# The V side of two more head pairs loaded row by row, in a fused attention and two-MLP kernel, with the attention list written anew

## The chip, the cores and the metric

The kernel runs on one core of a Trainium2 chip. The metric is the device time of one execution in microseconds, the median of several runs. One execution was also recorded by the hardware profiler, and every row shown below is from that one.

## The reference

Three stages follow one another; the change lies in the first. q, k and v have 2 batches, 8 heads, 768 positions and a head size of 64.

```python
k_sum = k.reshape(B, H, nb, 32, D).max(axis=3)       # 24 block summaries of the keys
v_sum = v.reshape(B, H, nb, 32, D).mean(axis=3)      # 24 block means of the values
scores_l = scale * q @ k^T                           # kept where |i - j| < 16
scores_s = scale * q @ k_sum^T + log(32)
a = softmax(concat([scores_l masked, scores_s]))
out = a @ concat([v, v_sum])
```

The result, as x of shape (2, 768, 512), goes through a token MLP over the 768 positions (`w_tok1`, 256 wide, and `w_tok2`), a channel MLP (512 to 1536 to 512), and then a layer norm with another channel MLP (512 to 2048 to 512), each with its residual.

## The kernel before, in words

**Pairs, windows and groups.** Two heads that follow one another make a pair; there are 8 pairs (i = 0 to 7; 0 to 3 are batch 0). A pair has 12 windows of 64 queries. A window sees 96 keys and 24 block summaries, 120 columns in all (`NK`). Four windows make a group; group n belongs to pair n // 3, so there are 24 groups.

**One group.** `q` (`att_qk`, L459) makes the scores on TensorE, 16 small matmuls; `m` (`att_min`, L479) adds the mask and takes the row minimum on VectorE, four instructions; `e` (`att_exp`, L500) is the exponential on ScalarE, four instructions; `t` (`att_tr`, L508) transposes the four probability blocks on TensorE; `c` (`att_evac`, L516) copies them out of PSUM on ScalarE; `a` (`att_av`, L522) multiplies them with V, 16 small matmuls; `n` (`att_norm`, L540) divides, on VectorE. All the scores live in one PSUM tile, of which groups of even and odd n use alternate strips.

**K.** `l` (`load_pair`, L322) loads K and Q of a pair. `k` (`prep_k`) takes the block maxima on VectorE; `K` copies them beside the keys with ScalarE, `J` does the same with GpSimd.

**V, first way, pairs below `NT`.** `v` (`load_vt`, L346) loads V with the head sizes on the partitions, 128 x 6 x 160, into a tile of `wide` (named VW). The block means are summed either by VectorE (`s`, L393 to L399) and written by ScalarE (`S`, L420 to L428), or summed by GpSimd (`p`, `sum_v`, L379) and written by GpSimd (`T`, `mean_v`, L409) or by ScalarE (`S`). Then TensorE turns the pair round in three groups `w` (`att_vtr`, L444) of four transposes each, and each group is copied out of PSUM into the tile V by ScalarE (`x`) or VectorE (`X`) (`att_vev`, L453).

**V, second way, the other pairs.** `r` (`load_v`, L352) loads V twice over with positions on the partitions, already cut into windows: two DMAs of 96 partitions x 6 x 136 numbers, with ones beside the values. `v` (L350) also loads the plain turned V, 128 x 768, into the tile VT. `s` (`prep_v1`, L400 to L407) sums the blocks there with GpSimd: four additions that halve the width, and two that write the sums into Z. `S` (L429, L430) is one transpose of Z on TensorE; `z` (`prep_v3`, L432) scales and copies it out with ScalarE into the single tile zs; `u` (`prep_v4`, L436) writes the means into the 12 windows of V with two GpSimd copies.

**Buffers.** V has three tiles (i % 3), K and Q three (i % 3), VT two (i % 2), zs one, and `stage`, into which `h` (`load_half`, L207) loads a weight block of 512 KB, three. `W` and `D` decode such a block (ScalarE, then VectorE), `C` and `O` split it into two halves. `g`, `G` and `H` are steps of the token MLP and of the transposes after it, which TensorE does between the groups; an entry `g` with a number below 4 or of 10, 11, 20 or 21 is 12 matmuls of 256 columns (`g1`, L556), and `g4` to `g9` are 12 matmuls of 512 columns each (`g2`, L575). `f` is a matmul on zeros, put in where nothing else can be done.

**The order.** `FRONT` (L49 to L63) is a list of such letters with their numbers. `attention` (L1119) walks it once, and each engine's instructions, the DMA queue of SyncE among them, keep the order of the list. So an entry that waits holds up all the later ones of its engine, and no engine's work moves past another entry of its own. When the list is through, the channel MLPs follow (`run`, from L1251).

Of the kernel before, what the change touches and what calls it, by code (L numbers as in the profile page):

```python
# [44 lines left out]
EARLY = 16  # L45
NEG = -8e9
EPS = 1e-9
NT = 4
FRONT = """  # L49
d0 f d1 f j0 f y0 f j1 f y1 f i0 v0 f i1 f l1 f K0 f v1 q0 l2 f f m0 f f e0 f h1 q1 t0 m1 f c0 f q2  # L50
e1 f m2 f l3 e2 t1 s0 f f f v2 t2 k1 S0 h2 w1 v3 w0 K1 x1 h0 q3 X0 c1 w2 m3 p1 a0 e3 q4 n0 c2 t3 m4
x2 a1 e4 k2 q5 T1 a2 n1 K2 c3 w3 m5 W1 t4 x3 D1 q6 c4 a3 e5 n2 w5 m6 w4 x5 t5 x4 n3 q7 p2 c5 k3 a4
e6 m7 a5 e7 t6 n4 r4 q8 n5 J3 S2 p3 t7 c6 m8 h4 w7 W2 y2 w6 X7 c7 q9 l4 e8 X6 a7 D2 v4 a6 S3 W0 v5
n7 w11 l5 w9 m9 x11 t8 x9 w8 D0 c8 q10 x8 w10 n6 e9 g1 X10 W4 k4 D4 K4 s4 t9 m10 C4 g0 c9 O4 G1 e10
H1 s5 q11 G0 H0 t10 l6 m11 S4 a8 e11 k5 q12 h3 z4 t11 c10 h7 n8 u4 a9 h5 m12 v7 e12 a10 n9 r5 J5 q13
n10 c11 t12 m13 a11 c12 k6 e13 q14 S5 a12 J6 m14 z5 e14 u5 t13 n12 q15 n11 c13 t14 W3 m15 a13 W7 D3
q16 e15 g2 m16 e16 s7 n13 D7 C3 c14 t15 O3 C7 q17 c15 t16 m17 G2 a14 e17 H2 q18 n14 r7 c16 a15 m18
e18 a16 l7 n15 q19 n16 W5 g3 h6 D5 v6 h8 m19 C5 h9 e19 r6 O5 t17 t18 G3 c17 q20 H3 k7 c18 g7 m20 K7
e20 g5 H7 W6 q21 H5 s6 g8 m21 e21 D6 S7 g6 W8 H8 h10 C6 D8 z7 t19 W9 u7 S6 g4 z6 O6 h11 H6 u6 q22 H4
g9 m22 e22 q23 H9 a18 m23 b g19 n18 g12 G19 a17 G12 H19 t20 H12 c19 g13 n17 c20 g16 t21 G16 a19 G13  # L60
H16 e23 a20 H13 n19 g11 c21 n20 t23 G11 g15 H11 t22 G15 g14 c22 H15 a21 G14 g18 c23 n21 a22 G18 H14
a23 n22 g10 n23 H18 g20 G10 H10 g21 G20 H20 P17 G21 G17 H21 H17
"""  # L63
SCALE = 1.0 / math.sqrt(D)

# [5 lines left out]
class Kern:  # L71
# [274 lines left out]
    def load_vt(self, i):  # L346
        if i < NT:
            self.nc.sync.dma_start(self.wide[i][:, 0:6, NB : NB + 160], self.vk[i])
        else:
            self.nc.sync.dma_start(self.VT[i % 2], self.vt[i - NT])  # L350

    def load_v(self, i):  # L352
        nc = self.nc
        if i < NT:
            return
        V = self.V[i % 3].rearrange("p (j w) c -> p j w c", j=2)
        nc.sync.dma_start(V[NB:NK, 0], self.v[i - NT, 0])
        nc.sync.dma_start(V[0:96, 1], self.v[i - NT, 1])

    def value(self, i, w):  # L360
        return self.V[i % 3][:, w if i < NT else 6 * (w % 2) + w // 2]

# [1090 lines left out]
```

## Time and profile before

| | |
|---|---|
| median of 3 runs | 559.36 us (558.47 to 559.53) |
| profiled execution | 558.98 us, its span 557.2 us |
| TensorE busy | 549.6 us (99%) |
| VectorE busy | 403.1 us (72%) |
| ScalarE busy | 272.3 us (49%) |
| GpSimd busy | 35.3 us (6%), all of it in the first 74 us |
| moved by DMA | 135.74 MB, mean 244 GB/s |
| granted TensorE clock | 1.00 of full speed |

Busy time of TensorE counts the pipelined length of each matmul, so two matmuls that overlap are busy once, and what one adds to the time is read from the start of one group to the start of the next.

### The profile page before, as it was taken

Reading aid. Unit: us, or ns where it says so; the run is one execution under the profiler, and the core shown is the slowest. Engines: PE = TensorE matmul, PEld = TensorE weight load, DVE = VectorE, ACT = ScalarE, POOL = GpSimd, SP = SyncE. Lnnn points to the kernel's source line nnn. Section 1 sums busy time; section 2 is a strip of 40 time slices with the busy share of each in tenths; the row PEclk is TensorE's granted clock in tenths of the full one; section 3 lists DMA queues with packets and bytes.
Section 4 is the critical chain, followed back from the end, with each engine's and each line's share of the span. In section 5 each row is a group of like instructions: output and inputs, shape, how many; then the busy total and the mean of one; then the engine's idle time right before and its main releaser. Section 6 shows DMA issues by size and latency. Waiting matters only on the chain.

```text
span 557.2 us, 10264 instructions
## 1 busy us (share of the span) xinstructions
PE 549.6 (99%) x3673; PEld 495.4 (89%) x3674; DVE 403.1 (72%) x977; ACT 272.3 (49%) x602; POOL 35.3 (6%) x66
## 2 busy tenths in 40 slices
PE   8999999999999999999999999999999999999997
PEld 4877779899899898999999998888998999999997
DVE  5989864657776887655669957888866776677781
ACT  5979653237754645454787325463422223334320
POOL 3554320000000000000000000000000000000000
PEclk9999999999999999999999999999999999999999
DMA  8977920425888879898656995897787898777555
GB/s 257 336 245 240 309 79 2 151 78 193 256 283 296 291 270 311 287 308 304 241 204 231 303 329 179 288 331 261 251 310 229 282 322 257 236 240 241 176 156 184
DMA packets 63810, 135.74 MB, mean 244 GB/s; under 512 B 5776, under 2 KB 23056, under 8 KB 63760
## 3 DMA queue, kind: packets, MB, share of 16 engines
q1 hardware_dynamic: 63760, 135.09, 72.8%
q8 instruction: 29, 0.48, 0.4%
q14 instruction: 21, 0.17, 0.1%
HBM read 100.47 MB, written 34.60 MB: 242 GB/s over the span
## 4 chain that ended last, share of the span: by engine, by line
PE 88%; DMA 4%; ACT 3%; POOL 2%; DVE 1%; issue 1%; SPq 0%; POOLq 0%; DVEq 0%; ACTq 0%
PE m L319 8%; PE m L318 8%; PE m L317 8%; PE acc_x L318 4%; PE acc_x L319 4%; PE acc_x L317 4%; PE g L560 3%; PE acc_y L319 2%; PE acc_y L318 2%; PE acc_y L317 2%; ACT pr L504 2%; DMA VT<-in_vt_dram 1%; DMA stage<-in_wts_dram 1%; PE acc_m L319 1%; PE acc_m L318 1%; PE acc_m L317 1%
## 5 line engine op out<-in xcount | busy, mean ns | idle before, releaser
L317 PE MATMUL m<-slot,slot 128*128 128x384 f32 (+1 forms) x136 | 45.8, 337 | 0.0
L319 PE MATMUL m<-slot,slot 128*128 128x384 f32 (+1 forms) x136 | 45.4, 334 | 0.0
L318 PE MATMUL m<-slot,slot 128*128 128x384 f32 (+1 forms) x136 | 45.4, 334 | 0.0
L319 PE MATMUL acc_x<-slot,al 128*128 128x512 f32 x96 | 37.8, 394 | 0.0
L318 PE MATMUL acc_x<-slot,ah 128*128 128x512 f32 x96 | 37.8, 394 | 0.0
L317 PE MATMUL acc_x<-slot,ah 128*128 128x512 f32 x96 | 37.5, 391 | 0.0
L504 ACT ACTIVATE pr<-sn,mn 128x120 f32<-128x120 f32 x96 | 29.8, 389 | 5.3 <-DVE mn L489 5.3
L317 PEld LDWEIGHTS m<-slot,slot 128*128 128x128 f32 x136 | 25.6, 188 | 1.8
L318 PEld LDWEIGHTS m<-slot,slot 128*128 128x128 f32 x136 | 25.6, 188 | 1.6
L165 DVE SCALAR_TENSOR_TENSOR dec<-stage,dec 128x512 uint32<-128x512 uint32 x36 | 25.1, 696 | 0.7
L319 PEld LDWEIGHTS m<-slot,slot 128*128 128x128 f32 x136 | 25.5, 188 | 0.0
L142 ACT ACTIVATE dec<-stage 128x512 f32<-128x512 f32 x36 | 24.3, 675 | 1.0 <-DMA stage<-in_wts_dram 1.0
L489 DVE CUSTOM_DVE_ANT_0 sn<-scores,mask 128x120 f32<-128x120 f32 x96 | 21.3, 277 | 3.7 <-DMA mask<-in_mask_dram 2.0
L560 PE MATMUL g<-u,tok 128*128 128x256 f32 x96 | 22.1, 383 | 0.0
L856 ACT ACTIVATE ah<-sm 128x384 fp32r<-128x384 f32 x16 | 8.4, 523 | 28.1 <-DVE sm L866 28.1
L688 ACT ACTIVATE f_B<-tx,gt 128x384 f32<-128x384 f32 x16 | 9.3, 582 | 25.4 <-PE tx L684 25.4
L319 PEld LDWEIGHTS acc_x<-slot,al 128*128 128x128 f32 x96 | 18.0, 188 | 4.0
L319 PE MATMUL acc_y<-slot,al_s 128*128 128x256 f32 x72 | 20.1, 280 | 0.0
L318 PE MATMUL acc_y<-slot,ah_s 128*128 128x256 f32 x72 | 20.1, 279 | 0.0
L560 PEld LDWEIGHTS g<-u,tok 128*128 128x128 f32 x96 | 17.8, 190 | 2.6 <-issue 0.3
L651 ACT ACTIVATE xn<-u,nb,rs 128x128 f32<-128x128 f32 x48 | 20.1, 482 | 0.0
L317 PE MATMUL acc_y<-slot,ah_s 128*128 128x256 f32 x72 | 20.0, 278 | 0.0
(1506 smaller groups left out, 1729.2 us busy)
## 6 DMA issues: line engine op xcount, KB each, us to landing
stage<-in_wts_dram SPq DMA_DIRECT2D x62, 512.0 KB, 4.4
slot<-w1s SPq DMA_DIRECT2D x94, 256.0 KB, 3.7
w1s<-sps SPq DMA_DIRECT2D x16, 512.0 KB, 4.6
w2s<-sp SPq DMA_DIRECT2D x16, 512.0 KB, 3.3
slot<-w2s SPq DMA_DIRECT2D x16, 512.0 KB, 4.7
w2t<-wk SPq DMA_DIRECT2D x16, 512.0 KB, 4.9
slot<-w2t SPq DMA_DIRECT2D x8, 768.0 KB, 5.2
slot<-w2s SPq DMA_DIRECT2D x22, 256.0 KB, 4.6
```

The lines of the kernel that those rows point to most:

```text
L142: fold = lambda out: nc.scalar.activation(out, high, AF.Prelu, scale=2.0**-112, alpha=-(2.0**32))
L165: put(m, t[:, :, 0], 29, m, op0=ALU.logical_shift_right, op1=ALU.bitwise_or)
L317: nc.tensor.matmul(out, lhs[0], rhs[0], start=first, stop=False)
L318: nc.tensor.matmul(out, lhs[0], rhs[1], start=False, stop=False)
L319: nc.tensor.matmul(out, lhs[1], rhs[0], start=False, stop=last)
L489: nc.vector.tensor_tensor_reduce(sn[:, u], ps[:, u % 2, u // 2, :NK], self.mask[:, mv], scale=-SCALE, scalar=3e38, op0=ALU.add, op1=ALU.mi ...
L504: self.nc.scalar.activation(self.pr[n][:, u], sn[:, u], AF.Exp, bias=mn[:, u : u + 1], scale=-1.0)
L560: nc.tensor.matmul(ps[:, :256], self.tok1(st, t), self.u[:, b * ST + st, 256 * hf : 256 * hf + 256], start=st == 0, stop=st == ST - 1,)
L651: nc.scalar.activation(xn[:, j], self.u[:, g * GT + j, cc * P : cc * P + P], AF.Identity, bias=nb[:, j : j + 1], scale=rs[:, j : j + 1],)
L688: nc.scalar.activation(x, ps[:, :GN], AF.Copy, scale=self.gt[:, cc : cc + 1])
L856: nc.scalar.activation(ah, x, AF.Relu)
```

## The change

`NT` goes from 4 to 2, so pairs 2 and 3 take the second way for V, and `FRONT` is another list. Gone from the list are `w6` to `w11` and their copies, `p2`, `p3` and the entries that served them; new are `r2`, `r3`, `s2`, `s3`, `z2`, `z3`, `u2`, `u3`; `S2` and `S3` stand for another thing, the transpose. `K1` and `K4` become `J1` and `J4`. The host's layout follows `NT`.

```diff
-NT = 4
+NT = 2
 FRONT = """
-d0 f d1 f j0 f y0 f j1 f y1 f i0 v0 f i1 f l1 f K0 f v1 q0 l2 f f m0 f f e0 f h1 q1 t0 m1 f c0 f q2
-e1 f m2 f l3 e2 t1 s0 f f f v2 t2 k1 S0 h2 w1 v3 w0 K1 x1 h0 q3 X0 c1 w2 m3 p1 a0 e3 q4 n0 c2 t3 m4
-x2 a1 e4 k2 q5 T1 a2 n1 K2 c3 w3 m5 W1 t4 x3 D1 q6 c4 a3 e5 n2 w5 m6 w4 x5 t5 x4 n3 q7 p2 c5 k3 a4
-e6 m7 a5 e7 t6 n4 r4 q8 n5 J3 S2 p3 t7 c6 m8 h4 w7 W2 y2 w6 X7 c7 q9 l4 e8 X6 a7 D2 v4 a6 S3 W0 v5
-n7 w11 l5 w9 m9 x11 t8 x9 w8 D0 c8 q10 x8 w10 n6 e9 g1 X10 W4 k4 D4 K4 s4 t9 m10 C4 g0 c9 O4 G1 e10
-H1 s5 q11 G0 H0 t10 l6 m11 S4 a8 e11 k5 q12 h3 z4 t11 c10 h7 n8 u4 a9 h5 m12 v7 e12 a10 n9 r5 J5 q13
-n10 c11 t12 m13 a11 c12 k6 e13 q14 S5 a12 J6 m14 z5 e14 u5 t13 n12 q15 n11 c13 t14 W3 m15 a13 W7 D3
-q16 e15 g2 m16 e16 s7 n13 D7 C3 c14 t15 O3 C7 q17 c15 t16 m17 G2 a14 e17 H2 q18 n14 r7 c16 a15 m18
-e18 a16 l7 n15 q19 n16 W5 g3 h6 D5 v6 h8 m19 C5 h9 e19 r6 O5 t17 t18 G3 c17 q20 H3 k7 c18 g7 m20 K7
-e20 g5 H7 W6 q21 H5 s6 g8 m21 e21 D6 S7 g6 W8 H8 h10 C6 D8 z7 t19 W9 u7 S6 g4 z6 O6 h11 H6 u6 q22 H4
-g9 m22 e22 q23 H9 a18 m23 b g19 n18 g12 G19 a17 G12 H19 t20 H12 c19 g13 n17 c20 g16 t21 G16 a19 G13
-H16 e23 a20 H13 n19 g11 c21 n20 t23 G11 g15 H11 t22 G15 g14 c22 H15 a21 G14 g18 c23 n21 a22 G18 H14
-a23 n22 g10 n23 H18 g20 G10 H10 g21 G20 H20 P17 G21 G17 H21 H17
+d0 f d1 f j0 f y0 f j1 f y1 f i0 v0 f i1 f l1 f K0 f v1 q0 f v2 f m0 f l2 f e0 f f q1 h1 t0 m1 f c0
+f f e1 q2 f m2 f l3 e2 t1 f s0 r2 c1 t2 k1 S0 w1 v3 J1 w0 x1 h2 q3 X0 a1 p1 m3 a0 e3 n1 q4 n0 c2 t3
+w2 m4 c3 s2 x2 k2 q5 e4 a2 m5 K2 t4 r3 n2 W1 q6 T1 e5 D1 S2 h0 w3 w5 z2 m6 h4 x3 u2 t5 c4 X5 a3 e6
+k3 q7 w4 c5 n3 J3 t6 x4 m7 a5 e7 a4 n5 s3 q8 c6 n4 t7 m8 a6 W2 q9 e8 D2 S3 v5 z3 m9 t8 c7 u3 l4 c8
+a7 n6 e9 q10 l5 n7 a8 m10 W0 t9 v4 e10 D0 q11 r5 c9 m11 t10 s5 e11 g0 h3 n8 r4 W4 k4 c10 h7 D4 l6 J4
+t11 G0 q12 C4 H0 v7 g1 O4 h5 m12 y2 e12 k5 s4 q13 G1 H1 a9 m13 a10 e13 n9 q14 J5 n10 c11 S4 t12 z4
+m14 t13 u4 c12 a11 e14 q15 n11 S5 c13 t14 m15 z5 g2 W3 u5 e15 D3 W7 C3 D7 t15 G2 q16 H2 C7 a13 O3
+a12 c15 m16 g3 s7 e16 n13 n12 c14 k6 W5 D5 q17 J6 G3 t16 H3 C5 a14 m17 a15 e17 r7 n14 q18 n15 c16
+t17 h8 m18 a16 c17 l7 e18 a17 n16 q19 v6 n17 t18 r6 m19 g11 e19 O5 h6 c18 h11 W8 g7 G11 D8 S7 t19 H7
+h10 z7 u7 q20 c19 H11 k7 g8 m20 K7 s6 e20 g5 H8 q21 H5 g6 m21 e21 S6 g4 H6 W6 z6 D6 u6 q22 H4 C6 h9
+g9 m22 e22 a19 H9 a18 n19 q23 n18 b g12 O6 g19 G12 t20 G19 H12 t21 c20 H19 g13 c21 m23 a20 G13 a21
+e23 H13 g16 n20 g18 G16 n21 t23 G18 t22 H16 c23 H18 g15 c22 a23 G15 W9 a22 H15 n23 g14 g10 n22 G14
+H14 g20 G10 H10 g21 G20 H20 P17 G21 G17 H21 H17
 """
```

## Rows read from the trace of the kernel before

**Rows 1.** Windows by stage: length, then busy time of each engine with its instructions.
```profile
core 0: us, PE busy (x) PEld busy (x) DVE busy (x) ACT busy (x) POOL busy (x), PEclk, DMA share, GB/s
...
40.00:54.00 14.00, 13.30 (x225) 10.25 (x217) 13.10 (x67) 12.48 (x36) 6.93 (x13) 1.00 0.77 251
54.00:74.00 20.00, 18.93 (x206) 14.50 (x206) 17.59 (x74) 12.98 (x36) 9.18 (x14) 1.00 0.82 262
...
93.10:557.20 464.10, 460.91 (x2580) 426.88 (x2579) 333.62 (x674) 208.58 (x431) 0.00 (x0) 1.00 0.74 248
```
**Rows 2.** Waits of TensorE to 93 us: total us, times, longest.
```profile
PE vtr L450 <- ACT VW L422: 0.9, 2, 0.8
PE scores L470 <- POOL VT L404: 0.7, 1, 0.7
PE psv L430 <- POOL Z L407: 0.6, 1, 0.6
```
**Rows 3.** Timeline of TensorE: start us, length, instruction, operands, count.
```profile
19.44 0.64 PE L470 MATMUL scores<-K,Q 64*64 64x120 f32 x16
...
25.45 1.09 PE L450 MATMUL vtr<-ident,VW 128*120 128x128 f32 x8
26.47 0.64 PE L470 MATMUL scores<-K,Q 64*64 64x120 f32 x16
...
29.07 1.09 PE L450 MATMUL vtr<-ident,VW 128*120 128x128 f32 x8 [0.75 <-ACT VW L422]
30.00 0.60 PE L513 MATMUL pt<-ident,pr 128*120 128x128 f32 x4
30.44 0.63 PE L450 MATMUL vtr<-ident,VW 128*120 128x128 f32 x4
30.99 0.64 PE L470 MATMUL scores<-K,Q 64*64 64x120 f32 x16
...
44.49 0.32 PE L430 MATMUL psv<-ident,Z 128*120 128x128 f32 x1
44.75 0.69 PE L532 MATMUL av<-V,PT 121*64 121x65 f32 x16
```
**Rows 4.** Timeline of GpSimd, 16 to 71 us.
```profile
16.81 0.63 POOL L410 TENSOR_SCALAR VW<-vs 128x168 f32<-128x168 f32 x1
...
34.53 3.03 POOL L404 TENSOR_TENSOR VT<-VT 128x384 f32<-128x384 f32 x4 [5.88 <-DMA VT<-in_vt_dram]
37.64 0.41 POOL L407 TENSOR_TENSOR Z<-VT 128x24 f32<-128x24 f32 x2
...
67.37 1.06 POOL L407 TENSOR_TENSOR Z<-VT 128x24 f32<-128x24 f32 x2
68.38 2.18 POOL L442 COPY V<-zs 24x768 f32<-24x768 f32 x2
```
**Rows 5.** Chain that ended last, 53 to 75 us: start, length, link.
```profile
56.12 8.14 DMA VT<-in_vt_dram
...
72.02 1.37 POOL V L442
...
73.43 0.68 PE av L532 x14
```
**Rows 6.** Timeline of SyncE's DMA queue.
```profile
53.54 0.31 SPq L357 DMA_DIRECT2D V<-in_v_dram  x1
```
**Rows 7.** Windows of 5 us, columns as in the first group.
```profile
30.00:35.00 5.00, 5.00 (x46) 4.26 (x45) 4.17 (x11) 3.94 (x11) 0.47 (x1) 1.00 1.06 379
35.00:40.00 5.00, 5.00 (x64) 4.01 (x66) 3.42 (x20) 3.80 (x12) 4.53 (x9) 1.00 0.19 68
```
**Rows 8.** Timeline of VectorE around 52 us.
```profile
51.23 0.69 DVE L243 TENSOR_TENSOR slot<-dec,slot 128x512 fp32r<-128x512 f32 x1
52.19 1.15 DVE L243 TENSOR_TENSOR slot<-dec,slot 128x512 fp32r<-128x512 f32 x1 [0.27 <-ACT slot L222]
53.26 0.27 DVE L489 CUSTOM_DVE_ANT_0 sn<-scores,mask 128x120 f32<-128x120 f32 x1
```

## Prediction

> **What bounds the kernel now.** I read the windows by stage first, since one share over the whole span would mix the attention with the MLPs [rows 1]. From 93 us to the end TensorE is busy 460.9 of 464.1 us, and the view of waits has no entry of TensorE for that stretch. So the MLPs run at TensorE's pace, and whatever the attention's end gains or loses comes out at the end of the kernel, one for one. Only the first 93 us need an argument. There TensorE is nearly full too: 13.3 of 14 us between 40 and 54, 18.9 of 20 between 54 and 74. VectorE stands beside it with 13.1 of 14 us in the first of these, so two engines are near their limit at once. The waits of TensorE came next [rows 2]: 0.9 us for the mean of a V tile, 0.7 for scores, 0.6 for the sums Z. Then its timeline, for what a step costs from start to start [rows 3]; then GpSimd's and the queue's, because the change moves work there [rows 4 to 7].
>
> The front is thus a sum: TensorE's work plus its waits. Work that leaves TensorE shortens it fully, if no new wait takes its place.
>
> **What is removed.** Six groups of four transposes go, w6 to w11. From start to start, w7 and w6 took 26.47 - 25.45 = 1.02 us, w11 and w9 30.00 - 29.07 = 0.93, w8 30.99 - 30.44 = 0.55 [rows 3]: 2.50 us for five, 0.5 each, so **-3.0 us** for six. Their copies out of PSUM (four on ScalarE, two on VectorE net) go too; what these free is counted below with the order. The wait of w11 for the mean of pair 3 has no successor of its kind, as there is no such mean to wait for: **-0.8** (the longer of the two waits of 0.9 in sum [rows 2]; the rest, before w1, stays).
>
> **What is added on TensorE.** Two transposes of Z, S2 and S3. One took 44.75 - 44.49 = 0.26 us [rows 3]: **+0.5**.
>
> **The last V of the chain.** The end of the front hangs on pair 6 before the change: its VT is issued at 56.12, takes 8.14 us to land, is summed, and its means reach V at 73.4, when a18 starts [rows 5]. The queue could not issue it sooner, because r7 ahead of it waited until 53.54 for a14 to free pair 4's V [rows 6]. In this chain u7 stands between the sums s6 and u6, and holds GpSimd for 2.18 us [rows 4]; zs has one buffer, so z6 waits for u7. The new list puts u7 ahead of s6, into the time in which pair 6's VT is on its way, and puts g11, 12 matmuls more, ahead of a18. The chain to a18 gets some 2 us shorter and its cover on TensorE longer. But S6 itself waits for Z, 0.6 us before [rows 2], and the sums up to Z are as long as they were; TensorE's entries between a14 and S6 sum to about what DMA and sums take. I take **-0.5**, between nothing and -0.8 (that wait and the 0.2 us that a18 waits).
>
> **What waits anew.** GpSimd's work is one queue, and two places of it are tight.
>
> First T1, the mean of pair 1, which w3 and w5 need. Before, it followed p1 at 16.81 [rows 4]. Now s2 stands ahead of it. One pass of sums takes 3.03 + 0.41 us [rows 4], so T1 runs from about 20.2 and ends at 20.9 (pass of 2.9 to 4.1 us: 20.3 to 21.5). TensorE gets through q6, which started at 19.44 [rows 3] and whose place hangs on VectorE as before, at 20.0, then S2 at 0.26; then w3 stands still: **+0.6**, between 0.1 and 1.3. Behind w3 are t5, a3 and q7; part of the delay may be hidden, as q7 also waits for m6 on VectorE, which T1 doesn't touch.
>
> Second J4, the key summary of pair 4, now on GpSimd behind s5, where before ScalarE wrote it. Only q12 and what follows it need it. The queue's bytes say when: v4 landed at 34.53 [rows 4] with 9.82 MB in the list up to it. In the new list 9.36 MB stand up to v5, so at 0.34 MB per us (between the mean up to that landing, 9.82 / 34.5 = 0.28, and the 0.38 of [rows 7]) it lands near 33.1, s5 ends at 36.6, J4 at 36.9. s4 then waits for v4, now behind 11.53 MB, 5.0 us later than before: 39.5, and S4 has its Z at 42.9. On TensorE q12 would be ready at about 36.5 and S4 at about 42.5. **+0.8** for both, between 0 and 2.
>
> The order on ScalarE adds a little: c4 stands behind x3, and a5 and a4 behind x4, all later because of T1: **+0.5**, between 0 and 1. VectorE gives back two copies of 0.6 us in the stretch in which q(n+1) always starts just after m(n): **-0.3**, between 0 and -1.2.
>
> **The DMAs.** A pair's V was 0.49 MB (128 x 960 numbers) and is now 0.39 + 0.63 MB (128 x 768, and twice 96 x 816): 1.06 MB more for two pairs, 2.8 us at 379 GB/s [rows 7]. That load is in a full stretch: a share of 1.06 between 30 and 35 us. But between 35 and 40 the queue moved only 68 GB/s, because it stood behind a K buffer; at full rate these 5 us hold 1.5 MB more. So the added bytes fill a hole, and what they delay is what was priced above; pair 2's rows stand at 6.38 MB in the list, 3 MB ahead of v5, so they land some 9 us before it, near 24; a6, behind q8 and t7, comes later than that.
>
> **Sum.** -3.0 - 0.8 + 0.5 - 0.5 + 0.6 + 0.8 + 0.5 - 0.3 = -2.2. I followed the new list down to a18 as well, entry by entry with these prices, and came to -3.3, as TensorE's entries fill some of these waits. I take -2.7. The profiled execution took 558.98 us, so **556.3 us**; the median of the runs shown, 559.36, lies 0.4 above it. With all gains at their large end and no new wait: -4.8, 554.2. With the new waits at their large ends: -3.0 - 0.8 + 0.5 + 1.3 + 2.0 + 1.0 = +1.0, 560.0.
>
> **Rivals.**
> *More than that.* The new order may take away waits that I left in: the 0.7 us of scores [rows 2], which came about because an operation of VectorE took 1.15 us for 0.69 [rows 8], and the short stops between groups. Removed work with no wait in its place: -3.0 - 0.8 + 0.5 - 0.8 - 0.7 = -4.8, half-way to it -4.3: 554.7 us. Chance 0.16.
>
> *GpSimd stops VectorE.* The slow operation of VectorE at 52.19 us reads two tiles of SBUF, and ran while GpSimd summed pair 7's VT; its twin a microsecond before took 0.69 [rows 8]. The change gives GpSimd some 5 to 6 us more of such work (two passes of sums of 3.4 us for two of 2.9, two pairs of copies of about 2, two key copies), in the stretch where VectorE has no room. Three such meetings on VectorE's path cost 3 x 0.46 = 1.4 us: -2.7 + 1.4, 557.7 us. For it speaks that row; against it, that m and n, most of VectorE's work here, read PSUM and one tile of SBUF, and the m at 53.26, beside the same GpSimd pass, took no longer than any other [rows 8]. Chance 0.10. [...]
>
> *The transposes lay beside the limit.* If the alternation of q on TensorE and m on VectorE sets the pace, groups w only filled its holes, as VectorE's 13.1 of 14 us suggest [rows 1]. Then only waits count: -0.8 - 0.5 + 0.6 + 0.8 = +0.1, 559.1 us. Against it: the w groups stand back to back with their neighbours, in a stretch in which TensorE had hardly a gap. Chance 0.14.
>
> *Slower: the queue before J4.* From r7's issue at 53.54 [rows 6] to the landing of pair 6's VT at 64.26 [rows 5], r7, l7, h6 and v6, 2.42 MB, took 10.7 us: 0.23 MB per us. If the row-wise rectangles of 96 partitions are the reason, and the stretch from r2 to v5, 3.6 MB, runs at that rate, v5 lands 3.6 / 0.23 - 3.6 / 0.34 = 5.1 us later, and J4 and q12 with it: -2.7 + 5.1 = +2.4, 561.4 us. It decides from about 2.7 us of delay at J4. Against it: r4, of the same kind, stood ahead of v4 in the queue, and v4's landing is one of those that gave the rate above; and at 53.5 us the queue had run empty, so its start is in the 10.7 us. Chance 0.10.
>
> **How the numbers follow.** My forecast has 0.50 (555.2 to 557.5). Against no change, about 0.2% or 1.1 us is what a measurement of this kernel can tell; 558.2 and 560.5 are those bounds. Faster: forecast, more, and GpSimd's stops, 0.76. Same: the transposes beside the limit, 0.14. Slower: 0.10. A range from 554.2 to 558.9 leaves out most of the last and the tail of the first.
>
> **What would show it.** Right: the first matmul of the channel MLP, at 93.1 us, starts near 90.4; no vtr after 26 us; TensorE waits once for T1's mean near 20.5 us; u7 ends before s6 starts, and a18 doesn't wait for V. Wrong: a wait of scores behind J4, or of psv behind s4, of over 2 us; VectorE operations of decoding at over 1 us in numbers; or a TensorE wait after 93 us, which would say that the front's gain was given back.

## The result, and the profile after

The changed kernel takes 562.63 us (median of 10 runs, 558.98 to 564.85), the kernel before 558.99 beside it (10 runs, 558.0 to 559.82): a ratio of 1.0057, 95% interval 1.0040 to 1.0074. It is slower by 0.6%, outside the predicted range. The profiled execution took 564.1 us with a span of 562.3; only two of the ten took longer, so the rows below explain 5.1 us, of which the medians show 3.6. The windows by stage, as in [rows 1], with the stretch around the change split out:

```profile
13.00:27.00 14.00, 13.14 (x237) 10.45 (x237) 12.38 (x62) 11.60 (x33) 8.22 (x16) 1.00 1.06 294
27.00:40.00 13.00, 8.36 (x113) 6.25 (x113) 6.58 (x39) 7.08 (x20) 8.04 (x14) 0.74 0.91 263
40.00:54.00 14.00, 13.13 (x161) 10.48 (x160) 11.32 (x51) 10.65 (x31) 6.79 (x12) 1.00 1.05 271
54.00:74.00 20.00, 19.27 (x243) 15.56 (x242) 16.53 (x69) 13.71 (x36) 5.24 (x9) 1.00 0.70 217
97.90:562.30 464.40, 461.17 (x2583) 427.13 (x2581) 333.68 (x674) 208.97 (x431) 0.00 (x0) 1.00 0.74 248
```

The same first two windows of the kernel before:

```profile
13.00:27.00 14.00, 13.90 (x258) 11.15 (x256) 12.67 (x67) 13.66 (x38) 7.46 (x15) 1.00 1.02 338
27.00:40.00 13.00, 12.25 (x151) 10.34 (x149) 10.52 (x41) 9.96 (x28) 6.49 (x12) 1.00 0.73 245
```

Read the last row of the first fence first: it begins with the first matmul of the channel MLP, at 97.90 us in TensorE's timeline. In that view of the kernel before it starts at 92.83, 5.1 earlier (the 93.1 of [rows 1] is the chain's start of it), and the spans differ by 562.3 - 557.2 = 5.1 as well. So the MLPs take as long as they did, and the loss lies ahead of them. Then find the row that stands out: between 27 and 40 us TensorE is busy 8.36 us against 12.25, and its granted clock is 0.74 of full speed. Third, look at the row above it: the DMA engines' share is as full as before (1.06 against 1.02), but they move 294 GB/s against 338. They are busy and get less done. The rows that follow trace the loss to that, and the experiments test it.

The waits of TensorE, 13 to 98 us, beside [rows 2], and its timeline at the longest (columns as in [rows 3]):

```profile
PE psv L430 <- POOL Z L407: 4.0, 2, 3.6
PE pt L513 <- ACT PT L520: 0.8, 2, 0.5
PE scores L470 <- issue: 0.7, 1, 0.7
```
```profile
28.81 0.44 PE L470 MATMUL scores<-K,Q 64*64 64x120 f32 x8 [0.70 <-issue]
32.82 0.47 PE L430 MATMUL psv<-ident,Z 128*120 128x128 f32 x1 [3.58 <-POOL Z L407]
33.66 1.11 PE L513 MATMUL pt<-ident,pr 128*120 128x128 f32 x4 [0.37 <-ACT zs L434]
34.70 1.14 PE L532 MATMUL av<-V,PT 121*64 121x65 f32 x16
```

S3, the new transpose of Z for pair 3, stands still for 3.58 us. The two groups behind it show a second cost: four transposes take 1.11 us where [rows 3] has 0.60, sixteen matmuls of av 1.14 where it has 0.69. The clock in windows of 1 us says why:

```profile
30.00:31.00 1.00, 0.00 (x0) 0.00 (x0) 0.00 (x0) 0.16 (x1) 0.84 (x3) 0.81 1.04 310
31.00:32.00 1.00, 0.00 (x0) 0.00 (x0) 0.44 (x2) 1.00 (x4) 0.84 (x3) 0.50 0.90 253
...
37.00:38.00 1.00, 1.00 (x19) 0.93 (x18) 0.98 (x9) 0.81 (x4) 0.92 (x2) 0.77 1.04 310
```

While TensorE stood, the granted clock fell to 0.50, and it came back in the window from 37 to 38. Who was late is in GpSimd's timeline and in the chain of waits:

```profile
20.27 0.79 POOL L410 TENSOR_SCALAR VW<-vs 128x168 f32<-128x168 f32 x1
...
29.13 2.48 POOL L404 TENSOR_TENSOR VT<-VT 128x384 f32<-128x384 f32 x4 [4.77 <-DMA VT<-in_vt_dram]
31.69 1.08 POOL L407 TENSOR_TENSOR Z<-VT 128x24 f32<-128x24 f32 x2
...
41.54 0.45 POOL L377 COPY K<-ks 128x168 f32<-128x168 f32 x1 [1.67 <-DVE ks L368]
```
```profile
15.35 13.70 DMA VT<-in_vt_dram
```

Pair 3's turned V (v3, 384 KB) was issued at 15.35 us and landed 13.70 us later; pair 6's, in [rows 5], took 8.14. It lies in the queue behind r2, pair 2's two row-wise loads. ScalarE was stopped by the next entry of the same queue, the weights h2: W2, which decodes them, waited for them, and e8 stands behind W2. SyncE itself was stopped by the sums s3, because v5 goes into the buffer that they read (the two fences):

```profile
30.84 0.66 ACT L142 ACTIVATE tok<-stage 128x512 f32<-128x512 f32 x1 [4.18 <-DMA stage<-in_wts_dram]
```
```profile
SPq L350 <- POOL Z L407: 3.7, 1, 3.7
```

So v5, which I had landing at 33.1 us, was issued at 32.80, and the copy J4 above ended at 41.99 in place of 36.9.

### The profile page after: what moved, and what is told of

It is laid out like the page before. It is cut to its first block, busy times and chain, and to the rows that moved or that the text cites. A ratio compares the mean times of both kernels' runs of the same rounds, so it can differ in the third digit from the quotient of the medians.

```text
span 562.3 us, 10228 instructions
## 1 busy us (share of the span) xinstructions
PE 549.8 (98%) x3651; PEld 494.1 (88%) x3652; DVE 402.5 (72%) x975; ACT 270.3 (48%) x596; POOL 38.4 (7%) x74
## 4 chain that ended last, share of the span: by engine, by line
PE 89%; DMA 6%; SPq 1%; ACT 1%; POOL 1%; DVE 1%; issue 0%; ACTq 0%; POOLq 0%
PE m L319 8%; PE m L318 8%; PE m L317 7%; DMA VT<-in_vt_dram 6%; PE acc_x L318 4%; PE acc_x L319 4%; PE acc_x L317 4%; PE g L560 3%; PE acc_y L319 2%; PE acc_y L318 2%; PE acc_y L317 2%; PE tu L605 1%; PE pt L513 1%; PE acc_m L319 1%; PE acc_m L317 1%; PE acc_m L318 1%
## 5 line engine op out<-in xcount | busy, mean ns | idle before, releaser
L165 DVE SCALAR_TENSOR_TENSOR dec<-stage,dec 128x512 uint32<-128x512 uint32 x36 | 25.8, 717 | 0.7
L142 ACT ACTIVATE dec<-stage 128x512 f32<-128x512 f32 x36 | 24.3, 675 | 2.2 <-DMA stage<-in_wts_dram 2.2
L169 DVE SCALAR_TENSOR_TENSOR dec<-stage,dec 128x512 uint32<-128x512 uint32 x23 | 15.8, 689 | 6.1 <-ACT stage L142 6.0
```

What stands on the lines that cost most here:

```text
L142: fold = lambda out: nc.scalar.activation(out, high, AF.Prelu, scale=2.0**-112, alpha=-(2.0**32))
L165: put(m, t[:, :, 0], 29, m, op0=ALU.logical_shift_right, op1=ALU.bitwise_or)
L169: put(m, t[:, :, 1], 3, m, op0=ALU.logical_shift_left, op1=ALU.bitwise_or)
```

## The experiments

Theory, after these rows: the row-wise rectangles (96 partitions x 816 numbers, line 357 and line 358) move slowly although all DMA engines are busy, and what stands behind them in the queue comes late: v3 for S3, h2 for W2, then v5. Rivals: the order of the queue alone (one late entry, one stop); the clock alone; the added bytes whatever their shape; the place of S3.

**The order of the queue.** Four versions move entries of the list.

`v3_first`: `s0 r2 ... w1 v3` becomes `s0 v3 r2 ... w1`.


> v3 goes into the DMA queue ahead of r2, nothing else. Theory A (two late loads stop TensorE together: v3 through S3 in TensorE's own queue to 32.8 us, h2 through W2, which stands ahead of e8 on ScalarE, to 31.4, so t8 to 32.7): v3 lands some 4 us earlier and S3 hardly waits, but h2's bytes stand where they did, so t8 waits on to about 32.5; the time falls by less than 1.5 us from 562.6. Theory B (S3 alone is the stop): the wait and the slow clock behind it go, 557 to 558.5.


Measured 561.23 us, ratio 1.0043 (1.0025 to 1.0061), as theory A had it. v3 was in time (the sums s3 began at 24.43 us in place of 29.13), and the weights were not:

```profile
29.97 0.68 ACT L142 ACTIVATE tok<-stage 128x512 f32<-128x512 f32 x1 [3.49 <-DMA stage<-in_wts_dram]
```

`w2_later`: `W2` goes behind `m10` in the list, `D2` behind `e10`.


> W2 and D2, the decoding of h2, move behind e9 and e10, in front of W0 and D0; the DMA queue as in the changed kernel. Theory A: S3 still waits for v3 near 32.8, so less than 1 us is won, 561.5 to 562.6. Rival (W2 holding up e8 is the stop, and S3's wait would be covered): 557 to 559.


Measured 563.41, ratio 1.0083 (1.0061 to 1.0105): the stop of W2 is gone and nothing is won. That is above both ranges that I had given. In the execution profiled, S3 waited for 1.2 us only, and the clock still fell: its mean was 0.71 from 27 to 34 us and 0.81 from 34 to 41.

`both`: the two edits together.


> v3 ahead of r2, and W2, D2 behind e9 and e10. Theory A: no stop of TensorE over 1.5 us between 26 and 34, no slow clock, time 556.5 to 558.5, under the kernel before. Rival C (the front's end is set elsewhere, by v5, which waits for s3, and r7 to VT of pair 6): TensorE's stop goes but comes back further on, and the time stays above 560.


Measured 561.80, ratio 1.0064 (1.0040 to 1.0088). My theory A failed and rival C came true: with both stops gone, others took their place further on. The waits of TensorE:

```profile
PE psv L430 <- POOL Z L407: 1.2, 1, 1.2
PE av L532 <- DMA V<-in_v_dram: 1.1, 1, 1.1
...
PE scores L470 <- POOL K L377: 0.4, 1, 0.4
```

Now a6 waits for pair 2's rows themselves, q12 for J4, S4 for its Z.

`reorder`: all of the queue from v3 to v4 in the order of need:

```diff
-r2 ... v3 ... h2 ... r3 ... h0 ... h4 ... v5 ... l4 ... l5 ... v4
+v3 ... h2 ... r2 ... h0 ... h4 ... l4 ... v5 ... r3 ... l5 ... v4
```


> The changed kernel with another order of the DMA queue and of nothing else: after l3 come v3, h2, r2, h0, h4, l4, v5, r3, l5, v4 (instead of r2, v3, h2, r3, h0, h4, v5, l4, l5, v4). The rows move no faster, but what is needed first comes first, and r3 comes behind l4. Theory D: W2 and S3 wait for less than 1 us, a6 for r2 perhaps 1 us, time 555.5 to 558. Rival G (the rows' slowness only moves the wait to l4 and r2): over 559.


Measured 561.46, ratio 1.0041 (1.0025 to 1.0056): rival G's side, over 559. One long wait is left and it is J4's:

```profile
PE scores L470 <- POOL K L377: 2.3, 1, 2.3
PE pt L513 <- ACT PT L520: 0.8, 2, 0.5
```

The four orders took between 561.2 and 563.4 us. Each time the wait moved to another entry of the queue, so the queue as a whole is late, not one entry of it.

**The clock.** `fill_wait` puts 16 matmuls on zeros ahead of S3, so that TensorE doesn't stand (15 of them are recorded below).


> 16 matmuls on zeros, 3.4 us, stand in TensorE's queue ahead of S3, and nothing else is changed; the wait itself stays. If the fall of the granted clock after the stop is a large part of the loss, the clock stays at 1.00 in all stretches and the time falls to 558.5 to 560.5. If the stop itself is the loss, the time stays within 1 us of 562.6. TensorE gets 3.4 us of work in a hole of 3.6, so it costs nothing where the hole is as long as in the profiled execution, and up to 1 us where it is shorter.


Measured 562.28, ratio 1.0067 (1.0044 to 1.0089), with the clock at 0.999 or 1.00 in all six runs. In its profiled execution pair 3's V landed in time, 20 to 27 us moved 284 GB/s (233 in the changed kernel's), and the fills simply cost their length:

```profile
28.03 0.44 PE L470 MATMUL scores<-K,Q 64*64 64x120 f32 x8 [0.33 <-issue]
28.63 3.40 PE L1180 MATMUL fill_ps<-warm 128*128 128x512 bf16 x15 [0.16 <-issue]
31.87 0.27 PE L430 MATMUL psv<-ident,Z 128*120 128x128 f32 x1
32.51 0.65 PE L513 MATMUL pt<-ident,pr 128*120 128x128 f32 x4 [0.37 <-ACT zs L434]
...
35.48 0.64 PE L470 MATMUL scores<-K,Q 64*64 64x120 f32 x16
```

So holding the clock up doesn't by itself bring the time back: six runs at full clock took 562.28 us against 562.63. How much the clock costs on top of the stop this run doesn't isolate: in the one execution profiled there was no stop to fill, and the fills put their own 3.2 us in its place. It shows, too, that one order of the loads is late in some executions and not in others. That may be why the changed kernel spreads over 5.9 us where the kernel before spreads over 1.8; the one of its ten runs whose mean clock was 1.00 took 558.98.

**The loads.** `rows_none` leaves r2 and r3 out: V of pair 2 is zeros, pair 3 has another pair's, so part of attention's result is missing.


> r2 and r3 are left out altogether; V of pair 2 holds zeros, of pair 3 the rows of pair 0, so attention's result for these pairs is left out. All theories: no wait for v3 or h2, time 555 to 557. If it were still over 558.5, the DMAs would have nothing to do with the loss, and it would lie in the order on the engines (rival F).


Measured 557.48, ratio 0.9974 (0.9962 to 0.9986): 1.5 us faster than before, and 0.5 slower than the top of what I had expected. This is what the change is worth without its row loads.

`rows_full` moves the same bytes as one DMA of 128 partitions x 1224 for each pair, into a spare tile.

```diff
+        if i < 4:
+            x = self.v[i - NT].rearrange("a p w c -> (a p w c)").rearrange("(p n) -> p n", p=P)
+            nc.sync.dma_start(self.scratch[i - 2], x)
+            return
```


> r2 and r3 move the same 627 KB each from the same place, but as one DMA of 128 partitions x 1224 numbers into a spare tile; V of pair 2 then holds zeros and of pair 3 the rows of pair 0, so attention's result for these pairs is left out. Theory D (a DMA into 96 partitions x 816 numbers moves at 150 to 280 GB/s and holds up all that stands behind it in the queue): the rate between 20 and 31 us stays over 330 GB/s, W2 and S3 no longer stop anything, the time falls to 555.5 to 557.5 with little spread. Rival E (1.06 MB more are too many for this stretch, in whatever shape): rate as high as that but v3 and h2 late by 2 us still, 558.5 or more.


Measured 557.65, ratio 0.9985 (0.9966 to 1.0003), just above theory D's range; eleven of the twelve runs lie between 556.6 and 559.7, and one took 562.89. The same bytes in the same place of the queue cost next to nothing (557.65 against 557.48), so it is not the bytes. That they go to a spare tile here is not the reason either: so do those of `rows_at0` below, which is slow.

`before_rows` is the other direction: the kernel before, with four such rectangles (1.25 MB) added behind v2 and v3, into tiles that nobody reads.


> The kernel before with four more DMAs, nothing else: two rectangles of 96 partitions x 816 numbers behind v2 and two behind v3, 1.25 MB into spare tiles that nobody reads. Theory D: the rate falls to 150 to 280 GB/s from about 21 us, v3, h2 and h0 come 3 to 6 us later, and the time grows by 2 to 5 us, to 561 to 564. If the time stays within 1 us of 559, the rows' DMAs cost nothing by themselves (rival F).


Measured 567.33, ratio 1.0143 (1.0123 to 1.0163), 8.2 us more and beyond what I had expected. Its windows and its longest wait:

```profile
20.00:27.00 7.00, 5.87 (x105) 4.88 (x102) 5.66 (x34) 5.73 (x18) 2.74 (x6) 1.00 1.07 250
27.00:34.00 7.00, 3.12 (x57) 2.58 (x56) 3.65 (x14) 2.64 (x7) 2.46 (x5) 0.80 1.06 213
```
```profile
PE vtr L455 <- ACT VW L427: 4.9, 2, 3.8
```

The loads alone, with nothing else of the change, lower the rate (250 GB/s from 20 to 27 us, before 307), stop TensorE and bring its clock down to 0.50 for a part of the second window.

**Which property of the loads.** One edit each: two DMAs of 128 partitions x 612 (`rows_two`: the number of DMAs is kept), and two of 96 x 816 that both begin at partition 0 (`rows_at0`: the number of partitions is kept, the odd start at 24 goes). Both leave out what `rows_none` does.

```diff
+            for a in range(2):                          # rows_two
+                nc.sync.dma_start(self.scratch[i - 2][:, 612 * a : 612 * a + 612], x[a])
+            for a in range(2):                          # rows_at0
+                nc.sync.dma_start(self.scratch[i - 2][0:96, 816 * a : 816 * a + 816], x[a])
```


> The changed kernel with the row-wise V of pairs 2 and 3 as two DMAs each of 128 partitions x 612 into a spare tile (the same bytes, the same number of DMAs, runs of 2.4 KB in place of 3.3); pair 2's V is zeros and pair 3's another pair's, so a part of attention's result is left out. If the number of partitions sets the rate: 20 to 27 us at 350 GB/s or more, no stop at the second token weights, 557.3 to 558. If the number of DMAs or their start does: 230 to 280 GB/s as in the changed kernel, and 561 to 563.

> As before it, with two DMAs of 96 partitions x 816, both of which start at partition 0 of a spare tile (in the changed kernel one starts at partition 24). The same part of attention's result is left out. If 96 partitions are slow wherever they begin: 20 to 27 us at 210 to 290 GB/s and 560.5 to 563. If only the one that starts at partition 24 is slow: 320 GB/s or more and 557.5 to 559.


Measured 558.11, ratio 0.9990 (0.9978 to 1.0001), and 562.56, ratio 1.0054 (1.0034 to 1.0074). Neither the start at partition 24 nor the number of DMAs is what makes the loads slow; what `rows_at0` and the changed kernel share is rows to 96 partitions. The DMA part of the page for 20 to 27 us (queue, packets, MB, time of the packets as a share of 16 engines), of the changed kernel, `rows_two`, `rows_at0` and `rows_full`:

```profile
q1 hardware_dynamic: 548, 1.60, 103.0%
```
```profile
q1 hardware_dynamic: 938, 2.68, 98.0%
```
```profile
q1 hardware_dynamic: 633, 1.81, 101.4%
```
```profile
q1 hardware_dynamic: 732, 2.65, 95.2%
```

Sixteen engines for 7 us are 112 us. In the changed kernel a packet took 1.03 x 112 / 548 = 0.21 us for 2.9 KB; in `rows_two` 0.98 x 112 / 938 = 0.12 us for 2.9 KB; in `rows_at0` 0.18 us, again for 2.9. These are means over all loads of the stretch. Sorted by size, the packet records of the same 7 us say more: in the changed kernel the rows' own packets (3264 B) took 255 ns on average, but the weights' packets (4096 B, over 128 partitions) took 249 ns, against 163 in `rows_two`, and packets of 3072 B 215 ns against 124; `rows_at0` has 234 and 186. So the rows slow the packets of the other loads that move beside them, by about half or more. With rows of 2.4, 4.9 and 6.5 KB over 128 partitions (`rows_two`, `rows_full`, and the next run) the stretch moved 387, 383 and 412 GB/s, and those of 3.3 KB, with which it moved 233 and 262 (the changed kernel and `rows_at0`), lie between them, so the length of a row is hardly it, though no run has just that length over 128 partitions. Why the packets slow down, no run here shows.

**A version to use.** `wide_rows` widens V to 128 partitions and loads a pair's rows, with the ones and the EPS row in place, as one DMA of 128 x 1632; `before_wide` does the same to the kernel before.

```diff
-        nc.sync.dma_start(V[NB:NK, 0], self.v[i - NT, 0])
-        nc.sync.dma_start(V[0:96, 1], self.v[i - NT, 1])
+        nc.sync.dma_start(self.V[i % 3], self.v[i - NT])
```


> The changed kernel with each pair's row-wise V as one DMA of 128 partitions x 1632 (836 KB, the columns of ones and the EPS row filled beforehand) instead of two of 96 x 816 (313 KB each): a third more bytes, the same computation. Theory (a DMA to 96 partitions moves slowly and holds up the list behind it): 20 to 27 us moves over 330 GB/s, pair 3's packed V lands before 26, TensorE stands less than 1 us for pair 3's sum and second token weights, and the time is 555.5 to 558. Rival (the bytes themselves, 1.25 MB more in the full stretch, are the loss): with 0.42 MB more for the two pairs it gets worse, 563 to 565.

> The kernel before with the same wide loads for the pairs that it loads row-wise (4 to 7), so that a gain of wide rows can be told from the gain of the change. Its TensorE had no stop that these loads made up to 53 us, so 0 to -0.5 from the kernel before (558.5 to 559.1). If it too falls to 557, wide rows are worth it by themselves and the change is worth the rest only.


Measured 558.99, ratio 1.0003 (0.9994 to 1.0013), and 558.59, ratio 0.9994 (0.9985 to 1.0004). A third more bytes than the narrow loads, and the loss of 0.6% is gone: 20 to 27 us moved 412 GB/s, W2 didn't wait. Yet it is no faster than before, and not in the 555.5 to 558 that I expected. The wide load writes the partitions into which u2 copies pair 2's means, so u2 has to wait for it (the profile of the next version names that wait), s3 stands behind u2 on GpSimd and began at 25.80 us, in `rows_full` at 23.76, and S3 stood for 1.3 us, with the clock near 0.50 from 31 to 34 us. For the kernel before, wide loads change nothing that can be measured.

So `wide_s3` moves S3, z3 and u3 behind q10 (nothing reads them before a9), and `s3_later` does that alone, with the narrow loads.

```diff
-D2 S3 v5 z3 m9 t8 c7 u3 l4 c8 a7 n6 e9 q10 l5 n7 a8
+D2 v5 m9 t8 c7 l4 c8 a7 n6 e9 q10 S3 l5 z3 n7 u3 a8
```


> The changed kernel with the wide row loads and, besides, S3, z3 and u3 five TensorE entries later in the list (S3 behind q10 in place of ahead of v5): nothing before a9 reads pair 3's means. If the stop ahead of S3 (1.3 us, and 3.3 us at half clock behind it in the profiled execution) is what wide rows alone still lost against the kernels without row loads: no psv wait over 0.5 us, granted clock 1.00, 557.3 to 558.3. If the wide loads' bytes, or the wait of u2 for them, are what is lost: 558.7 to 559.3 as before it.

> The changed kernel with only S3, z3 and u3 moved as in the run beside it; the row loads stay 96 partitions wide. By theory D the queue is as slow as before, so W2 (4.2 us late) still holds up ScalarE and the stop moves to a6, q12 or J4: 560.5 to 562.5. If the place of S3 alone were the mistake: 557.3 to 558.5.


Measured 558.94, ratio 1.0000 (0.9990 to 1.0010), and 561.32, ratio 1.0047 (1.0031 to 1.0064). The second lies in its range and answers its question: with narrow loads and S3 later, TensorE waits for e8, which stands behind W2.

```profile
PE pt L513 <- ACT pr L504: 2.2, 1, 2.2
```

The first doesn't do what I had hoped: by its time it is on the side of the wide loads' bytes, or of u2's wait for them, and no run separates the two. Its profiled execution (558.08 us) has no wait at S3 and u2 still waits for the rows:

```profile
22.99 1.71 POOL L440 COPY V<-zs 24x768 f32<-24x768 f32 x2 [2.65 <-DMA V<-in_v_dram]
```

Four of its 12 runs have a mean clock of 0.996 or 0.997 and take 559.4 to 559.8, so some runs of it still stand somewhere; which wait, a profile of another run doesn't tell. What the wide loads still cost against `rows_none`, about 1.5 us, is open. No version that computes everything beat the kernel before.

## Why the prediction was wrong

**The bound: right.** The MLPs pass the front's change on, and TensorE has no wait in them.

**What is removed: right in kind, too large in size.** Half of the 48 vtr transposes are gone, and with no row loads the whole change gives -1.5 us. My sum, -2.2, was nearer to that than the -2.7 that I took from following the list by hand. TensorE's windows from the start to the first matmul of the channel MLP, before, in the changed kernel and in `rows_none`, say what the work that left is worth:

```profile
0.00:92.83 92.83, 88.44 (x1093) 68.20 (x1095) 69.45 (x303) 63.49 (x172) 35.34 (x66) 1.00 0.68 220
0.00:97.90 97.90, 88.63 (x1072) 66.93 (x1073) 68.86 (x301) 61.35 (x166) 38.37 (x74) 0.97 0.76 220
0.00:92.18 92.18, 86.93 (x1072) 65.64 (x1073) 69.22 (x301) 61.05 (x166) 38.48 (x75) 1.00 0.71 219
```

In `rows_none`, at full clock as before, TensorE was busy 1.5 us less (1.6 and 2.0 less in `rows_two` and `rows_full`), where my starts of groups had promised 3.0 - 0.5 = 2.5. It was idle 0.9 us more. So the transposes did lie on the path, with some two thirds of their price, and the rival that put them beside the limit falls. "No successor" to w11's wait holds there too: S3 starts at 27.84 us without a wait. In the changed kernel S3 stands 3.58 us for its Z, which is the loads' doing and not counted in my sum.

**T1: right.** Its mean came at 20.27 + 0.79 = 21.06 us, and w3 started at 21.11, 0.45 after S2 in place of 0.26: 0.2 us of the 0.6, inside its bounds.

**The last V of the chain: right.** u7 ended at 72.7, before s6 began at 74.40, and no a18 waits for V; S6 waits 0.5 us for its Z, as I had left it. What the order is worth, my -0.5, no run isolates.

**Not told apart:** the order on ScalarE (+0.5) and the two copies fewer on VectorE (-0.3). No run isolates them.

**GpSimd stops VectorE: not put to the test.** Five decoding operations of VectorE up to 95 us took 682 to 693 ns; before, one took 1.15 us [rows 8]. But none of the five had GpSimd's work beside it for more than its last 0.2 us, so they speak neither for this rival nor against it.

**The DMAs: here it failed**, and with it J4's term (0.8, at most 2; `reorder`, where no long wait is in front of it, has 2.3). "The added bytes fill a hole" took the rate of a full stretch of wide loads (379 GB/s in [rows 7]) for loads of another shape, and took a hole at 35 to 40 us for room for loads that stand in the queue at 14 to 24. The loads of one queue are issued in order, so bytes put in at 14 us delay what stands behind them at 14 us (with v3 ahead of r2, s3 began 4.7 us sooner); a later hole gives nothing back. I asked of the delay only where it would meet pair 4 (v5 and J4), and not who stands right behind r2: v3 for S3, h2 for W2 and e8. At my rate of 0.34 MB per us v3, 0.39 MB behind the rows that I put near 24, would have landed near 25; it landed at 29.05. And v5 had a second condition that I missed, the buffer of V that s3 still reads. The slower rival had the mechanism, the rate (0.23 MB per us; 233 GB/s measured from 20 to 27 us) and nearly the time, 561.4, but the wrong place, and I gave it 0.10 on the ground that r4 had stood ahead of v4 in the list whose mean rate I used: a mean over 34 us hides three at a lower rate. Finer windows of the kernel before show r4 passing, at issue from 23.28 us:

```profile
23.00:24.00 1.00, 1.00 (x30) 0.93 (x27) 1.00 (x10) 1.00 (x5) 0.84 (x3) 1.00 1.06 390
24.00:25.00 1.00, 1.00 (x21) 0.69 (x20) 0.93 (x6) 1.00 (x5) 0.84 (x4) 1.00 0.81 229
25.00:26.00 1.00, 1.00 (x9) 0.89 (x10) 1.00 (x9) 1.00 (x4) 1.00 (x2) 1.00 0.65 199
26.00:27.00 1.00, 1.00 (x21) 0.71 (x19) 0.84 (x4) 1.00 (x3) 0.84 (x3) 1.00 0.86 251
```

These rows alone leave it open, since the share falls as well. The packet records lean one way: the weights' packets of 4096 B took 219 ns on average from 24.3 to 28.5 us, 179 from 20 to 23. So r4 seems to have slowed what moved beside it in the kernel before too, though less than r2 and r3 did in the changed one.

**The sum after.** Up to the first matmul of the channel MLP TensorE is idle 97.90 - 88.63 = 9.3 us, 4.9 more than before. It is busy 88.63 - 88.44 = 0.2 more, although work left: against the 86.5 to 86.9 us of the three runs at full clock above, the slow clock adds about 1.7 to 2.2. Of these the rows show 1.6: the five groups from 33.66 to 38.27 took 4.6 us, and in `fill_wait`, at full clock, 35.48 - 32.51 = 3.0. So -1.5 to -2.0 for the work, +1.7 to +2.2 for the clock and +4.9 for waits make the 5.1 by which the span grew.

**The low end.** The range's -4.8 "with all gains at their large end" is added up short: its terms, with VectorE's -1.2, give -5.3. Nothing hangs on it.

## What to carry to other kernels

Price a new load by the rate of loads of its own shape, read in windows as short as the load, and where none stands alone, measure one: the stretch with rectangles of 96 partitions moved here at two thirds of the rate that it had with the same bytes over 128 (262 against 387 GB/s). In a queue that is issued in order, list what stands behind the new load and when each is needed; a hole further on is no room. If reordering only moves the wait, as in the four orders here (561.2 to 563.4 us), the queue is the bound, and the shape of its entries is the next thing to try.

## What the runs showed of the hardware

A DMA share of 1.0 doesn't say that the DMAs move what they can: 20 to 27 us ran at a share of 1.04 and 233 GB/s in the changed kernel, and at 1.02 and 412 GB/s with wide loads. A load's shape also set the pace of others: in those 7 us packets of 4096 B to 128 partitions took 249 ns with rows to 96 partitions beside them, and 163 with the same bytes over 128 (`rows_two`). The rate of one and the same order of loads also varied between executions (233 and 284 GB/s in the changed kernel and in `fill_wait`). TensorE stood from 29.24 to 32.82 us; its granted clock was 0.81 in the window from 30 to 31 us, 0.50 in each from 31 to 37 and 0.77 in the next, and at 0.50 its groups took about 1.7 times as long (1.11 us for 0.65).
